# Nine score tiles turned by VectorE and a DRAM trip instead of TensorE, in a bucketed-attention and mixture-of-experts kernel

## The chip, the cores and the metric

The kernel runs on one core of a Trainium2 chip. The metric is device time in microseconds (us) of one execution, lower is better. The engines are named as the profile names them: PE is TensorE (PEld its weight load), DVE is VectorE, ACT is ScalarE, POOL is GpSimd, and SP is SyncE, whose queue issues nearly every DMA of this kernel. Each engine works through its own instructions in order.

## The reference

Two layers follow each other. The first is attention with a hash mask: a query sees only those keys whose six sign bits under a random projection are the same as its own. The second is a mixture of four experts over the attention's output, all experts computed for all rows and weighted by given probabilities.

```python
# q, k, v: (2, 8, 768, 64); proj: (64, 6); w1: (4, 512, 1024); w2: (4, 1024, 512)
q_bits = (np.einsum('bhsd,dk->bhsk', q, proj) > 0).astype(np.int64)
k_bits = (np.einsum('bhsd,dk->bhsk', k, proj) > 0).astype(np.int64)
q_bucket = np.sum(q_bits * powers, axis=-1)
k_bucket = np.sum(k_bits * powers, axis=-1)
mask = q_bucket[:, :, :, None] == k_bucket[:, :, None, :]
scores = np.where(mask, scale * np.matmul(q, k.transpose(0, 1, 3, 2)), -1000000000.0)
attn = np.exp(scores - np.max(scores, axis=-1, keepdims=True))
attn = attn / (np.sum(attn, axis=-1, keepdims=True) + 1e-09)
attn_out = np.matmul(attn, v)
...
x = attn_out.transpose(0, 2, 1, 3).reshape(B * S, H * D)
for e in range(E):
    h = np.maximum(x @ w1[e], 0.0)
    out += p[:, e:e + 1] * (h @ w2[e])
```

## The kernel before

**Tiles and steps.** There are 16 heads, (batch 0, heads 0 to 7) and then (batch 1, heads 0 to 7). A head's 768 queries are six tiles of 128. The attention is a software pipeline with one step per tile: at step i the tile i is scored, and operations on earlier tiles follow with fixed lags. In the text, t0 to t5 are the six steps in which a head's own tiles are scored. Inside a step the operations are written in the order T X S U V M E Y N R P:

- S (`stage_s`): four score matmuls on PE into a PSUM tile `sps` (two buffers), then on DVE a reduction over the scores (L432) that also writes them to the SBUF tile `p`.
- E, one step later: the exponential on ACT (L448).
- T, three steps after S (`stage_t`): the tile is turned by six 128x128 PE transposes (L493) into two PSUM tiles `ptps`; the first half is copied to SBUF by ACT (L499), the second by DVE where the tile is first or third of its group (L497), otherwise by ACT. Three tiles make a group, g = 0 and g = 1.
- X and Y, two and four steps after S (`stage_x`, `stage_y`): the other way to turn a tile. DVE transposes 32x32 blocks of the tile (L512), after three tiles one DMA writes the group (1152 KB) to a DRAM scratch `scr` (L518), and four DMAs of 288 KB read it back into `pt` in the wanted order (L529). SP waits for the write to land before it issues the reads.
- V (`stage_v`): the product with v, 12 matmuls (L547), in two parts of six pairs for a head of batch 0, at the lags LAG_V (4 and 6 steps after the head's last tile). Both groups of the head have to be there for either part.
- U: PSUM to SBUF by ACT (g = 0, L574) and DVE (g = 1, L572). N and R: reciprocals of the row sums on DVE, sent through DRAM (`row`) and spread over partitions into `rdb` (L473, one buffer, shared by a pair of heads). M (`stage_m`): three POOL operations per group on a pair's result: multiply by `rdb` (L585), then split into two float32r parts (L587, L590).
- P: steps of the generator `prep_head` for the next head: "hi" on ACT (L354) with copies on POOL (L242), "lo" on DVE (L357), "hash" on PE (`hps`, L369) with signs on ACT and two POOL copies (L384, L242). Loads of a later head's q, k (L216) and v (L232) and DVE's turn of a loaded q, k tile (L312) also stand here.

**Which way a tile goes.** `heavy(b, h, t)` chooses T for every tile of batch 0 and X and Y for every tile of batch 1.

**Stages.** Batch 0's attention runs first, beside the split of the first expert weights (casts L729 on DVE, subtractions L719 on POOL), which is paced by counting the yields of the attention generator. When batch 0 is done (126 us), PE goes over to the expert layers, and batch 1's attention is fed in between them. All PSUM tiles but `sps` share four buffers of one kind.

Of the kernel before, what the change touches and what calls it, by code (L numbers as in the profile page):

```python
# [21 lines left out]
SPLIT_AT = (1, 0)  # L22
# [9 lines left out]
LAG_M = (10, 10)  # L32
# [11 lines left out]
PREP_AT = 0  # L44
ORDER = "TXSUVMEYNRP"
LIGHT_FROM = 8
DRAIN = 2000
SPLIT_FIRST = 3
FAST = 6
# [3 lines left out]
def tile_lsh_attention__then__domain_moe(  # L53
# [24 lines left out]
    G = 3  # L78
# [235 lines left out]
    def prep_head(b, h):  # L314
        second = (b, h) == (0, 1)
        q1, al, ah, k2 = stack_tiles(b, h)

        def copies():
            for rows in (slice(0, D), slice(D, P)):
                copy_pool(q1[rows], ah[0:D].bitcast(F32))  # L320
            copy_pool(k2[0:D], ah[D:P].bitcast(F32))

        if second:
            for ps, sl in zip(in_psum, halves):
                nc.scalar.activation(ah[:, sl], ps[:, :NH], ACTF.Copy, scale=qk_scale)
            copies()
            yield 654
            for ps, sl in zip(in_psum, halves):
                low_half(al[:, sl], ps[:, :NH], ah[:, sl])
            yield 0  # L330
            yield 0
            ps = [one("hps1") for _ in range(2)]
            for j, (w, a) in enumerate(((phi, ah), (plo, ah), (phi, al))):
                for i, sl in enumerate(halves):
                    nc.tensor.matmul(ps[i][:MKE, :NH], w, a[:, sl], start=j == 0, stop=j == 2)
            copy_pool(ah[0:D], al[D:P].bitcast(F32))
            for i, sl in enumerate(halves):
                nc.scalar.activation(
                    k2[D:MKE, sl], ps[i][D:MKE, :NH], ACTF.Sign, bias=sgn_bias[D:MKE], scale=SGN_SCALE
                )  # L340
            yield 978
        else:
            xt = xts.pop((b, h))
            late = b * H + h > H
            steps = {}
            steps.setdefault(SPLIT_AT[late], []).append("hi")
            steps.setdefault(SPLIT_AT[late] + 1, []).append("lo")
            steps.setdefault(HASH_AT[late], []).append("hash")
            for at in range(max(steps) + 1):
                if at:  # L350
                    yield 654 if at == 1 else 0
                for what in steps.get(at, ()):
                    if what == "hi":
                        nc.scalar.activation(two(ah), two(xt), ACTF.Copy, scale=qk_scale)  # L354
                        copies()
                    elif what == "lo":
                        nc.vector.scalar_tensor_tensor(  # L357
                            out=two(al),
                            in0=two(xt),
                            scalar=qk_scale,  # L360
                            in1=two(ah).bitcast(F32),
                            op0=ALU.mult,
                            op1=ALU.subtract,
                        )
                        copy_pool(ah[0:D], al[D:P].bitcast(F32))
                    else:
                        hps = one("hps")
                        for i, sl in enumerate(halves):
                            nc.tensor.matmul(  # L369
                                hps[i * D : i * D + MKE - D, :NH],  # L370
                                pf[:, : MKE - D],
                                xt[:, sl],
                                start=True,
                                stop=True,
                                tile_position=(0, i * D),
                            )
                        for i, sl in enumerate(halves):
                            rows = slice(i * D, i * D + MKE - D)
                            nc.scalar.activation(
                                k2[D:MKE, sl], hps[rows, :NH], ACTF.Sign, bias=sgn_bias[rows], scale=SGN_SCALE  # L380
                            )
            if late:
                yield 978
        nc.gpsimd.tensor_scalar(  # L384
            out=al[D:MKE],
            in0=k2[D:MKE].bitcast(F32),
            scalar1=1.0,
            scalar2=bit_mul[D:MKE],
            op0=ALU.add,
            op1=ALU.mult,  # L390
        )
        copy_pool(k2[MQ:MQE], al[MK:MKE].bitcast(F32))
        yield 0 if second or b * H + h > H else 978
# [20 lines left out]
    def mixed(b, h):  # L414
        return b * H + h < LIGHT_FROM

    def heavy(b, h, t):
        return mixed(b, h)

    def stage_s(b, h, t):  # L420
        q1, q2, k1, k2 = heads[b, h]
# [177 lines left out]
    ready = [False]  # L599

    def v_lags(b, h):
        return LAST_V if (b, h) == (0, H - 1) else LAG_V[not mixed(b, h)]

    def u_lag(b, h):
        return v_lags(b, h)[-1] + (1 if (b, h) == (0, H - 1) else LAG_U[not mixed(b, h)])
# [4 lines left out]
    def attention():  # L610
        n = len(seq)
        prep = [iter(())]

        def do(op, i):
            if op == "N":
                j = i - LAG_N
                if 0 <= j < n:
                    stage_n(*seq[j])
            elif op == "R":
                for b in range(B):  # L620
                    for odd in range(2):
                        j = i - LAG_R[b][odd]
                        if 0 <= j < n and (seq[j][0], seq[j][1] % 2) == (b, odd):
                            stage_r(*seq[j])
            elif op == "T":
                j = i - LAG_T
                if 0 <= j < n and heavy(*seq[j]):
                    stage_t(*seq[j])
                    return 654
            elif op == "X":  # L630
                j = i - LAG_X
                if 0 <= j < n and not heavy(*seq[j]):
                    stage_x(*seq[j])
            elif op == "Y":
                j = i - LAG_Y
                if 0 <= j < n and j % G == G - 1 and not heavy(*seq[j]):
                    b, h, t = seq[j]
                    stage_y(b, h, t // G)
            elif op == "S":
                if i < n:  # L640
                    b, h, t = seq[i]
                    if t == 0:
                        x = hseq.index((b, h))
                        prep[0] = prep_head(*hseq[x + 1]) if x + 1 < len(hseq) else iter(())
                    stage_s(b, h, t)
                    return 652 + 4270 // NT
                return DRAIN
            elif op == "V":
                for bh, lag in ended(i):
                    for part, at in enumerate(v_lags(*bh)):  # L650
                        if lag == at:
                            stage_v(*bh, part, len(v_lags(*bh)))
                            if (bh, part) == ((0, H - 1), len(v_lags(*bh)) - 1):
                                ready[0] = True
                                return 0
            elif op == "U":
                for bh, lag in ended(i):
                    if lag == u_lag(*bh):
                        stage_u(*bh)
            elif op == "M":  # L660
                for (b, h), lag in ended(i):
                    for g in range(NT // G):
                        if h % 2 and lag == (u_lag(b, h) if (b, h) == (0, H - 1) else LAG_M[b] + g):
                            stage_m(b, h, g)
                if done_b[0] and ready[0]:
                    ready[0] = False
                    return 0
            elif op == "E":
                j = i - LAG_E
                if 0 <= j < n:  # L670
                    stage_e(*seq[j])
            elif op == "P":
                if i < n:
                    b, h, t = seq[i]
                    c = next(prep[0], None) if t >= PREP_AT else None
                    x = hseq.index((b, h))
                    if t == NT - 1 and x + 2 < len(hseq) and in_blocks(*hseq[x + 2]):
                        turn_blocks(*hseq[x + 2])
                    if t == QK_AT and x + 2 < len(hseq):
                        load_qk(*hseq[x + 2])  # L680
                    if t == NT - 1 and x + 1 < len(hseq):
                        load_v(*hseq[x + 1])
                    return c
            return None

        for i in range(n + LAG_M[1] + 3):
            for op in ORDER:
                c = do(op, i)
                if c is not None:
                    yield c  # L690
# [501 lines left out]
```

## Time and profile before

| what | value |
|---|---|
| median of 3 runs | 710.5 us (710.23 to 711.04) |
| the profiled execution's own time | 710.34 us |
| its span in the trace | 708.6 us |
| PE busy, share of the span | 700.9 us, 99% |
| DVE busy | 490.2 us, 69% |
| ACT busy | 333.6 us, 47% |
| POOL busy | 316.5 us, 45% |
| mean granted PE clock | 0.999 |

The shares are means over two stages with different work. PE's busy time counts matmuls that overlap each other, so 99% does not say that none of them waited. 1.7 us of the execution lie outside the span.

### The profile page before, as it was taken

The page shows a single profiled execution, that of the slowest core. Times are in us where ns is not written, and L with a number is a line of the kernel's source. Part 1 is how long each engine was busy: PE and PEld are TensorE (multiplying, and loading weights), DVE is VectorE, ACT ScalarE, POOL GpSimd, SP SyncE. Part 2 cuts the span into 40 slices and gives each one's busy share as a digit, 9 for nine tenths or more (in the row PEclk, how much of TensorE's full clock was granted, in tenths as well). Part 3 has the DMA queues.
Part 4 walks back from the last instruction along what each step waited for, and adds up shares of the span by engine and source line. Part 5 has one row for each costly group of instructions (what it writes and reads, how often), then busy time and mean ns, then how long its engine had stood idle before and what let it go on. Part 6 is the DMA issues. An engine that isn't in the chain of part 4 may idle for free.

```text
span 708.6 us, 10175 instructions
## 1 busy us (share of the span) xinstructions
PE 700.9 (99%) x3726; PEld 593.9 (84%) x3726; DVE 490.2 (69%) x782; ACT 333.6 (47%) x655; POOL 316.5 (45%) x290
## 2 busy tenths in 40 slices
PE   8999999999999999999999999999999999999997
PEld 6766675878887978978888989899898989989896
DVE  6898888865585754755228797886857667685762
ACT  6887788543453544524234444343433434353340
POOL 6359578523352453503238555543514234341420
PEclk9999999999999999999999999999999999999999
DMA  6323354768997977867931121421212121122202
GB/s 150 68 47 75 75 116 84 216 170 204 264 247 225 238 182 223 238 214 231 237 105 60 61 89 54 153 63 60 93 57 90 46 75 59 61 90 59 90 1 89
DMA packets 90848, 87.76 MB, mean 124 GB/s; under 512 B 53168, under 2 KB 55728, under 8 KB 90800
## 3 DMA queue, kind: packets, MB, share of 16 engines
q1 hardware_dynamic: 89776, 86.80, 44.2%
q8 instruction: 29, 0.48, 0.3%
q10 hardware_dynamic: 1024, 0.33, 0.2%
q14 instruction: 19, 0.16, 0.1%
HBM read 65.04 MB, written 22.07 MB: 123 GB/s over the span
## 4 chain that ended last, share of the span: by engine, by line
PE 93%; DVE 2%; POOL 2%; issue 1%; ACT 1%; DMA 0%; POOLq 0%; DVEq 0%
PE mps L760 12%; PE mps L762 12%; PE mps L761 12%; PE pv L547 8%; PE mps L808 5%; PE mps L810 5%; PE mps L809 5%; PE sps L427 4%; PE sps L425 4%; PE ptps L493 4%; PE mps L1051 3%; PE mps L1050 3%; PE mps L1047 3%; PE pa L1050 2%; PE pa L1051 2%; PE pd L1051 2%
## 5 line engine op out<-in xcount | busy, mean ns | idle before, releaser
L760 PE MATMUL mps<-w2hi,hh 128*128 128x512 f32 (+1 forms) x388 | 151.0, 389 | 0.0
L761 PE MATMUL mps<-w2lo,hh 128*128 128x512 f32 (+1 forms) x388 | 150.5, 388 | 0.0
L762 PE MATMUL mps<-w2hi,hl 128*128 128x512 f32 (+1 forms) x388 | 150.4, 388 | 0.0
L1033 POOL TENSOR_TENSOR w2lo<-ws,w2hi 128x512 fp32r<-128x512 f32 x40 | 50.7, 1287 | 124.0 <-ACT w2hi L1032 121.1
L432 DVE TENSOR_SCALAR_CACHE_REDUCE p<-sps 128x768 f32<-128x768 f32 x96 | 90.0, 939 | 17.8 <-PE sps L427 16.3
L754 DVE SCALAR_TENSOR_TENSOR acc<-mps,pe,acc 128x512 f32<-128x512 f32 (+1 forms) x85 | 62.9, 740 | 56.0 <-PE mps L762 55.7
L448 ACT ACTIVATE p<-p,nb 128x768 f32<-128x768 f32 x96 | 89.5, 933 | 23.4 <-DVE p L432 23.0
L762 PEld LDWEIGHTS mps<-w2hi,hl 128*128 128x128 f32 x388 | 72.9, 188 | 15.7
L760 PEld LDWEIGHTS mps<-w2hi,hh 128*128 128x128 f32 x388 | 72.8, 188 | 15.0 <-issue 1.2
L761 PEld LDWEIGHTS mps<-w2lo,hh 128*128 128x128 f32 x388 | 72.9, 188 | 14.0
L547 PE MATMUL pv<-pt,tv 128*64 128x384 f32 x288 | 67.1, 492 | 0.0
L992 POOL TENSOR_TENSOR w1lo<-ws,w1hi 128x512 fp32r<-128x512 f32 x30 | 47.5, 1589 | 41.9 <-ACT w1hi L988 41.7
L808 PE MATMUL mps<-xs,w1hi 128*128 128x384 f32 x192 | 65.1, 339 | 0.0
L810 PE MATMUL mps<-xs,w1lo 128*128 128x384 f32 x192 | 64.5, 336 | 0.0
L809 PE MATMUL mps<-xs,w1hi 128*128 128x384 f32 x192 | 64.5, 336 | 0.0
L843 ACT ACTIVATE hh<-mps 128x384 fp32r<-128x384 f32 x48 | 23.4, 489 | 84.6 <-PE mps L810 84.6
L1060 ACT ACTIVATE hh<-mt 128x384 fp32r<-128x384 f32 x60 | 31.5, 525 | 58.4 <-DVE mt L1105 38.0
L844 DVE SCALAR_TENSOR_TENSOR hl<-mps,hh 128x384 fp32r<-128x384 f32 x48 | 26.4, 554 | 46.0 <-ACT hh L843 45.7
L425 PE MATMUL sps<-ah,q 128*128 128x384 f32 x192 | 53.5, 359 | 0.4 <-DVE p L432 0.4
L547 PEld LDWEIGHTS pv<-pt,tv 128*64 128x64 f32 x288 | 24.9, 136 | 32.2 <-issue 30.7
L512 DVE STREAM_TRANSPOSE t<-p 128x768 f32<-128x768 f32 x48 | 46.3, 965 | 7.7 <-ACT p L448 7.6
L242 POOL TENSOR_SCALAR q<-ah 64x768 fp32r<-64x768 f32 (+1 forms) x33 | 27.1, 821 | 54.5 <-ACT ah L354 40.1
(160 smaller groups left out, 1528.6 us busy)
## 6 DMA issues: line engine op xcount, KB each, us to landing
ws<-in_moe_w_dram SPq DMA_DIRECT2D x64, 512.0 KB, 3.9
scr<-t SPq DMA_DIRECT2D x16, 1152.0 KB, 7.5
pt<-scr SPq DMA_DIRECT2D x64, 288.0 KB, 5.7
tv<-in_v_dram SPq DMA_DIRECT2D x16, 192.0 KB, 4.5
tqk<-in_q_dram SPq DMA_DIRECT2D x30, 96.0 KB, 3.3
out_dram<-acc SPq DMA_DIRECT2D x11, 256.0 KB, 2.0
tqk<-in_k_dram SPq DMA_DIRECT2D x28, 96.0 KB, 3.1
rdb<-row SPq DMA_DIRECT2D x14, 192.0 KB, 6.4
```

The source lines that it names most:

```text
L425: nc.tensor.matmul(ps[:, i, :NH], q1[:, sl], k1[:, i * NH : (i + 1) * NH], start=True, stop=False)
L432: nc.vector.tensor_scalar(out=two(pt), in0=ps[:, :, :NH], scalar1=MASKED, scalar2=MASKED, op0=ALU.min, op1=ALU.min, accum_out=nb,)
L448: nc.scalar.activation(pt, pt, ACTF.Exp, bias=nb, scale=-1.0, accum_out=dens[b, h, r][:, o : o + 1])
L547: nc.tensor.matmul(dst, vvs[b, h][:, c], pts[b, h, g][c], start=c == 0, stop=c == NT - 1, tile_position=(0, g * D),)
L754: nc.vector.scalar_tensor_tensor(out=acc, in0=ps, scalar=pcol, in1=acc, op0=ALU.mult, op1=ALU.add)
L760: nc.tensor.matmul(ps, hh[:, ts], w2hi[:, f, cs], start=n == 0, stop=False)
L761: nc.tensor.matmul(ps, hh[:, ts], w2lo[:, f, cs], start=False, stop=False)
L762: nc.tensor.matmul(ps, hl[:, ts], w2hi[:, f, cs], start=False, stop=n == FC - 1)
L808: nc.tensor.matmul(ps[:, :SB], w1hi[:, kk, fs], xhi[b, kk][:, sl], start=kk == 0, stop=False)
L809: nc.tensor.matmul(ps[:, :SB], w1hi[:, kk, fs], xlo[b, kk][:, sl], start=False, stop=False)
L810: nc.tensor.matmul(ps[:, :SB], w1lo[:, kk, fs], xhi[b, kk][:, sl], start=False, stop=kk == KD - 1)
L1033: nc.gpsimd.tensor_tensor(out=lo[:, c + o], in0=t[:, o], in1=hi[:, c + o].bitcast(F32), op=ALU.subtract)
```

## The change

In batch 0's heads 1, 3 and 5 the first group (tiles 0 to 2) goes by X and Y, the way of batch 1; their second group and all other heads stay with T. For these three heads the two parts of V move from 4 and 6 to 6 and 8 steps after the head's last tile, U follows at 11 instead of 9, and M at 11 and 12 instead of 10 and 11. For the head prepared during one of them (heads 2, 4 and 6), "hi" and "lo" come one step earlier, in t0 and t1.

```diff
+BY_BOTH = (1, 3, 5)
+LATE_V = (6, 8)
+LATE_M = 11
...
-            steps.setdefault(SPLIT_AT[late], []).append("hi")
-            steps.setdefault(SPLIT_AT[late] + 1, []).append("lo")
+            at = 0 if by_both(b, h - 1) else SPLIT_AT[late]
+            steps.setdefault(at, []).append("hi")
+            steps.setdefault(at + 1, []).append("lo")
...
+    def by_both(b, h):
+        return b == 0 and h in BY_BOTH
+
     def heavy(b, h, t):
-        return mixed(b, h)
+        return mixed(b, h) and not (by_both(b, h) and t < G)
...
     def v_lags(b, h):
+        if by_both(b, h):
+            return LATE_V
         return LAST_V if (b, h) == (0, H - 1) else LAG_V[not mixed(b, h)]
+
+    def m_lag(b, h):
+        return LATE_M if by_both(b, h) else LAG_M[b]
...
-                        if h % 2 and lag == (u_lag(b, h) if (b, h) == (0, H - 1) else LAG_M[b] + g):
+                        if h % 2 and lag == (u_lag(b, h) if (b, h) == (0, H - 1) else m_lag(b, h) + g):
```

Three places show how instructions move. Line numbers of the changed kernel are 3 to 12 higher than those of the kernel before, and numbers at a name's end are buffer numbers. The first place is PE in head 3, from the hash matmuls of t3 to the scores of t5, before:

```order
L369 MATMUL hps<-xt,pf 44x384 x2
L493 MATMUL ptps<-ident,p 128x128 x6
L425 MATMUL sps<-ah,q_540 128x384 x2
L427 MATMUL sps<-k_543,al 128x384 x2
L493 MATMUL ptps<-ident,p 128x128 x6
L425 MATMUL sps<-ah,q_540 128x384 x2
L427 MATMUL sps<-k_543,al 128x384 x2
```

The same place in the changed kernel:

```order
L373 MATMUL hps<-xt,pf 44x384 x2
L432 MATMUL sps<-ah,q_520 128x384 x2
L434 MATMUL sps<-k_523,al 128x384 x2
L432 MATMUL sps<-ah,q_520 128x384 x2
L434 MATMUL sps<-k_523,al 128x384 x2
```

The two sixes of transposes are gone (a third, ahead of t3, too), and three groups of score matmuls come close together.

The second place is DVE in head 3, from the second reduction (t1) to the fourth (t3), before:

```order
L432 TENSOR_SCALAR p,nb<-sps 128x768
L497 COPY pth<-ptps 128x3x128
L432 TENSOR_SCALAR p,nb<-sps 128x768
L729 CAST w1hi<-ws 128x512
L572 COPY xr<-pv 64x384
L459 TENSOR_SCALAR den<-den 128x6
L460 RECIPROCAL rd<-den 128x6
L357 SCALAR_TENSOR_TENSOR al<-xt,qk_scale,ah 128x768
L497 COPY pt<-ptps 128x3x128
```

In the changed kernel DVE has from there to the reduction of t5 (t_739 is the tile `t1` of `stage_x`):

```order
L361 SCALAR_TENSOR_TENSOR al<-xt,qk_scale,ah 128x768
L504 COPY pth<-ptps 128x3x128
L519 STREAM_TRANSPOSE t_739<-p 128x6x4x32
L439 TENSOR_SCALAR p,nb<-sps 128x768
L466 TENSOR_SCALAR den<-den 128x6
L467 RECIPROCAL rd<-den 128x6
L519 STREAM_TRANSPOSE t_739<-p 128x6x4x32
L439 TENSOR_SCALAR p,nb<-sps 128x768
L741 CAST w1hi<-ws 128x512
L519 STREAM_TRANSPOSE t_739<-p 128x6x4x32
L439 TENSOR_SCALAR p,nb<-sps 128x768
L579 COPY xr<-pv 64x384
```

A block transpose now stands ahead of each of three reductions, "lo" stands a step earlier, and the two copies of this group are gone.

The third place is the queue of SP between two loads of q and k, at the end of head 3, before:

```order
L462 DMA row<-rd 128x6
L473 DMA rdb<-row 64x768
L232 DMA tv<-in_v_dram 128x384
L708 DMA ws<-in_moe_w_dram 128x2x512
L216 DMA tqk<-in_q_dram 32x24x32 x2
```

The same place in the changed kernel:

```order
L469 DMA row<-rd 128x6
L525 DMA scr<-t_739 128x4x576
L480 DMA rdb<-row 64x768
L235 DMA tv<-in_v_dram 128x384
L536 DMA pt<-scr 32x4x576 x4
L219 DMA tqk<-in_q_dram 32x24x32 x2
```

The write of the group stands ahead of the DMA into `rdb`, the four reads behind it and behind the load of v; the load of expert weights has moved away from here.

## Rows read from the trace of the kernel before

**Rows 1.** Page, part 2: busy tenths in 40 equal slices.

```profile
PE   8999999999999999999999999999999999999997
...
DVE  6898888865585754755228797886857667685762
```

**Rows 2.** Windows, one per head from its first scores: heads 2, 3, 4; mean of 1 to 7.

```profile
core 0: us, PE busy (x) PEld busy (x) DVE busy (x) ACT busy (x) POOL busy (x), PEclk, DMA share, GB/s
...
32.11:45.74 13.63, 13.63 (x91) 9.49 (x89) 12.57 (x25) 11.36 (x25) 6.64 (x8) 1.00 0.28 60
45.74:59.38 13.64, 13.64 (x91) 9.49 (x90) 12.44 (x25) 11.49 (x25) 8.92 (x9) 1.00 0.19 29
59.38:73.64 14.26, 13.91 (x92) 9.46 (x90) 11.10 (x21) 11.32 (x25) 11.61 (x12) 1.00 0.48 122
...
sum 96.58, PE 95.97 PEld 66.41 DVE 83.70 ACT 79.78 POOL 62.17; mean PE 13.71 PEld 9.49 DVE 11.96 ACT 11.40 POOL 8.88
```

**Rows 3.** Timeline of PE, head 3 and start of head 4: start, us, line, count.

```profile
49.24 0.96 PE L493 MATMUL ptps<-ident,p 128*128 128x128 f32 x6
49.97 0.60 PE L425 MATMUL sps<-ah,q 128*128 128x384 f32 x2
...
50.84 0.54 PE L547 MATMUL pv<-pt,tv 128*64 128x384 f32 x1
...
52.82 0.82 PE L369 MATMUL hps<-xt,pf 128*44 128x384 f32 x4
53.57 0.87 PE L493 MATMUL ptps<-ident,p 128*128 128x128 f32 x6
54.20 0.59 PE L425 MATMUL sps<-ah,q 128*128 128x384 f32 x2
...
54.98 1.05 PE L493 MATMUL ptps<-ident,p 128*128 128x128 f32 x6
55.78 0.60 PE L425 MATMUL sps<-ah,q 128*128 128x384 f32 x2
...
60.33 0.62 PE L427 MATMUL sps<-k,al 76*128 76x384 f32 x2 [0.35 <-POOL k L242]
```

**Rows 4.** Groups of lines by form, 10 to 140 us: count | busy, mean ns | idle before.

```profile
L499 ACT ACTIVATE pth<-ptps 128x384 f32<-128x384 f32 x32 | 14.7, 487 | 8.5 <-PE ptps L493 8.5
...
L497 DVE COPY pt<-ptps 128x384 f32<-128x384 f32 x16 | 8.8, 553 | 0.2
...
L512 DVE STREAM_TRANSPOSE t<-p 128x768 f32<-128x768 f32 x7 | 6.7, 961 | 0.0
```

**Rows 5.** Timeline of DVE, head 3: the reduction of t4.

```profile
55.18 0.96 DVE L432 TENSOR_SCALAR_CACHE_REDUCE p<-sps 128x768 f32<-128x768 f32 x1 [0.46 <-PE sps L427]
```

**Rows 6.** Timeline of PE, head 4: the scores of t5.

```profile
70.03 0.60 PE L425 MATMUL sps<-ah,q 128*128 128x384 f32 x2
```

**Rows 7.** Timeline of SP: the first two trips through scr, of batch 1.

```profile
126.77 0.38 SPq L518 DMA_DIRECT2D scr<-t  x1
...
132.74 1.75 SPq L529 DMA_DIRECT2D pt<-scr  x4
136.84 0.38 SPq L518 DMA_DIRECT2D scr<-t  x1
...
144.43 1.74 SPq L529 DMA_DIRECT2D pt<-scr  x4
```

**Rows 8.** Line L529, 130 to 140 us, then 140 to 150 us: issue to landing.

```profile
DMA to landing us min/median/max: 3.2/4.5/5.7
...
DMA to landing us min/median/max: 4.4/5.6/6.5
```

**Rows 9.** Timelines of POOL and SP, end of head 3: a pair's multiplications and rdb.

```profile
61.60 1.20 POOL L585 TENSOR_TENSOR xr<-xr,rdb 128x384 f32<-128x384 f32 x1
...
51.90 0.33 SPq L462 DMA_DIRECT2D row<-rd  x1
62.82 0.48 SPq L473 DMA_DIRECT2D rdb<-row  x1
```

## Prediction

> **What bounds the kernel now.** I read the page by slices first. PE is at 9 tenths in nearly every slice; DVE stands at 8 or 9 tenths in the first seven slices, some 125 us, and at 5 to 8 later [rows 1]. The change is in that first stage, batch 0's attention, so I cut it by heads. A head takes 13.80 us on average (96.58 over seven heads), PE is busy in practically all of it, and DVE in 11.96, which leaves DVE 1.84 us of idle time per head; the granted clock is 1.00 throughout [rows 2]. The timeline of PE shows what a head is made of. The six transposes of one tile take 0.63 to 0.80 us from their start to the next scores; one half of the product with v takes 1.98 us (50.84 to 52.82), the hash matmuls 0.75 [rows 3]. So PE sets the pace of this stage, and DVE is second with 13% to spare. Behind the stage PE goes on into the expert layers at 9 tenths of every slice, so time saved ahead of them should come out at the end.
>
> **The change, part by part.**
>
> *PE loses nine sets of six transposes.* In head 3 the three that go are 49.24 to 49.97, 53.57 to 54.20 and 54.98 to 55.78: 0.73 + 0.63 + 0.80 = 2.16 us [rows 3]. Heads 1 and 5 have the same pattern, so PE loses about 6.5 us. Moving V removes nothing from PE: it stands two steps later, in t5 of the following head and t1 of the one after. A pair of heads (an odd one and the even one that follows) takes 27.6 us now and would be 25.4 for PE alone.
>
> *ACT loses copies.* Four copies per group at 0.487 us go, 1.9 us per odd head [rows 4]. ACT is not the bound (11.4 of 13.8 us [rows 2]), so I count nothing.
>
> *DVE gains.* It gets three block transposes of 0.961 us and loses two copies of 0.553: +1.78 us per odd head [rows 4]. The block transpose of batch 0 is not in this trace; that of batch 1 has the same form, and I take it unchanged. The pair needs 2 x 11.96 + 1.78 = 25.7 us of DVE [rows 2, 4]. That is more than PE's 25.4: the limit moves from one engine to the other, and of the 2.16 us that PE gives up at most 27.6 - 25.7 = 1.9 can be had per pair, 5.7 in all.
>
> *What the coupling takes.* That floor holds only if DVE never idles. It does idle whenever PE stands in V or hash and neither of the two score tiles in PSUM is waiting for it. Bounds: no idle time, and twice that of the head where DVE is densest now, head 2 with 13.63 - 12.57 = 1.06 us [rows 2]. With "lo" and the reductions placed as in the order above, DVE has work queued during most of PE's long blocks, so I take the middle, 1.06 us per pair: 26.76, a gain of 0.83 per pair and 2.5 us for three. The two ends give 5.7 and, at 2.1 us of idle time, -0.6.
>
> *"hi" and "lo" a step earlier, M a step later.* DVE's work does not change by it, only its place. On POOL it puts the copies of head 4's k ahead of the multiplications of heads 0 and 1. Now PE waits for that copy at the start of head 4, 0.35 us of it seen as idle time [rows 3], and head 4 takes 0.62 us more than head 3 [rows 2]. I count 0.5 us gained; 0 to 0.62 is possible.
>
> *The trip through DRAM.* This is new in this stage, with a wait that PE can feel: the matmuls of V need the read-back tile, and behind them in PE's order stand the next head's transposes and scores, on which DVE waits. Time available: the third block transpose stands ahead of the reduction of t4, which is at 55.18 now [rows 5]; V will stand behind the scores of t5 of the next head, at 70.03 + 0.87 (the distance of 49.97 to 50.84 [rows 3]) = 70.9 [rows 6]. From these 15.7 us go one half of V that moves out of the stretch (1.98), one set of transposes (0.80) and the wait for POOL (0.5): 12.4, and up to 1 us less when DVE runs late. I take 12. Time needed: from the issue of the write to the reads' issue 5.97 us (126.77 to 132.74) in the one trip that meets little other traffic, 7.6 in the next one (136.84 to 144.43) [rows 7]; then 1.75 us for four issues, of which the slowest lands 5.7 and 6.5 us after its own issue [rows 8]. That makes 11.7 to 13.4 us for the first trip, as the slowest is the first or the last of the four, and 14.1 to 15.8 for the second. Stage one moves less (DMA share 0.19 to 0.48 [rows 2]), so the first trip is the nearer one: V comes out just in time or a little late. One thing is worse than in batch 1: in SP's queue the DMA into `rdb` stands between write and reads, and it has to wait until POOL has multiplied the pair before. Now that wait holds SP from 52.2 to 62.82, until the multiplication that starts at 61.60 is done [rows 9]. Head 1 has no pair before it, so nothing; heads 3 and 5 I give 0.5 us each, -1.0 in all. The bounds are 0 and 3.8 (15.8 against 12) per head.
>
> *The other DMAs* (one write and four reads per odd head, ahead of a load of q and k that is needed a head later) cost SP 0.38 + 1.75 us of issue [rows 7], in a queue that stands idle for 10 us [rows 9]: nothing.
>
> **Sum.** 2.5 + 0.5 - 1.0 = 2.0 us off the profiled execution's 710.34 (span 708.6, with 1.7 outside it): 708.3. The median of the runs is 0.16 above that execution, so 708.4 for the median.
>
> **A rule that speaks against it.** In the rows, a tile's turn costs PE 0.63 to 0.80 and DVE 0.37 on average by the old way, and DVE 0.96 by the new one. The Trainium skill ("VectorE: DVE Perf Modes", section "Rules for kernel authors") advises TensorE for a 128x128 transpose whose result may go to PSUM, and DVE's transpose only inside 32x32 blocks. Taken as the deciding rule, the work would stay on PE, and the change would give nothing or lose; that is the first rival, whose price follows from the rows.
>
> **Rivals.**
>
> 1. *DVE takes it all.* If DVE keeps about the idle time that it has now around PE's long blocks, two times 0.95 us per pair instead of 1.06, a pair takes 25.7 + 1.9 = 27.6, as before, and the kernel 710.4, within 0.2% (1.4 us, about what a measurement of this kernel can tell from no change). For it: DVE and PE would be within 0.3 us of each other, and only two score tiles lie between them. Against: today's 1.84 us per head arises while DVE waits for a slower PE, which it then would not.
> 2. *The product with v waits for its tile.* Slower from the point where the wait is over 1 us per head (three heads against 2.5 + 0.5 gained). If `rdb` holds the reads back as it holds SP now and the reads meet traffic as in the second trip, the wait is 2 to 3.8 us per head; with 2.5 on three heads, 7.5 - 3.0 = 4.5 slower, 715; with 2.5 on heads 3 and 5 alone, 2.0 slower, 712.5. For it: 12 against 11.7 leaves nothing in reserve. Against: the earlier "hi" brings POOL's copies out of the way of the multiplication.
> 3. *The trip is hidden and DVE does not idle.* Then 5.7 + 0.5 are gained: 704.3. For it: the odd and even heads would be balanced on both engines. Against: an idle time of zero is in no window of the stage.
>
> **How the numbers follow.** The forecast (a gain of 0.5 to 4 us) gets 0.50, the first rival 0.25, the second 0.17, the third 0.08. A quarter of the forecast's weight lies under 1.4 us, and a little of the first rival's above: faster by over 0.2% 0.52, within 0.2% 0.28, slower 0.20. The range reaches down to most of the third case and up to the mild form of the second: 704.9 to 711.9; the forecast's own is 706.4 to 709.9.
>
> **What would show it.** In the profile after, the windows by head should give about 26.8 us for a pair, DVE busy in over 95% of it, and PE's score matmuls waiting for DVE's reduction (L439). The wait of head 4's score matmuls for POOL should be gone. The waits of PE's weight loads for V (L554) should name a DMA from `scr` for 0 to 1 us in heads 3 and 5 and none in head 1. The prediction is wrong if that wait is over 1 us per head, if a pair takes over 27.3 with DVE short of 95%, or if the expert stage, from its first matmul to the end, gets longer by what the first stage gave.

## The result and the profile after

The changed kernel takes 720.7 us (median of 4 runs, 720.40 to 721.26); the kernel before took 710.5 on the same chip. The ratio is 1.0143, with a 95% interval of 1.0126 to 1.0161. The forecast was 708.4 us with a range of 704.9 to 711.9: it is 12.3 us too low, and the kernel moved the other way. The profiled execution took 720.91 us, its span is 719.2.

Line numbers of the changed kernel are 3 to 12 higher than before: S is L432 and L434, the reduction L439, T L500, the block transpose L519, the write to `scr` L525, the reads L536, V L554, `rdb` L480, POOL's multiplication L592.

The page's slices (40 of 18 us) of PE and of its granted clock already have the place:

```profile
PE   8997979999999999999999999999999999999997
...
PEclk9998989999999999999999999999999999999999
```

PE falls to 7 tenths in the fourth and sixth slice, and the clock behind it, in the fourth and sixth too. The windows by head, which answer to [rows 2], say which heads (here heads 3 to 7, and the sum over 1 to 7):

```profile
core 0: us, PE busy (x) PEld busy (x) DVE busy (x) ACT busy (x) POOL busy (x), PEclk, DMA share, GB/s
...
44.05:57.73 13.68, 13.68 (x86) 8.43 (x84) 13.26 (x25) 10.03 (x21) 7.98 (x8) 1.00 0.40 103
57.73:76.40 18.67, 13.42 (x79) 9.24 (x78) 12.75 (x23) 11.38 (x25) 14.13 (x15) 0.82 0.76 162
76.40:89.98 13.58, 13.58 (x86) 8.46 (x84) 12.14 (x23) 9.93 (x21) 6.52 (x7) 1.00 0.66 167
89.98:108.93 18.95, 14.51 (x79) 9.88 (x77) 13.01 (x26) 11.59 (x25) 14.29 (x15) 0.83 0.69 141
108.93:125.62 16.69, 15.84 (x103) 10.43 (x101) 11.75 (x24) 11.67 (x25) 9.38 (x11) 0.99 0.29 56
sum 106.90, PE 94.99 PEld 63.73 DVE 86.63 ACT 75.96 POOL 63.24; mean PE 13.57 PEld 9.10 DVE 12.38 ACT 10.85 POOL 9.03
```

The sum was 96.58: these seven heads account for 10.3 of the 10.6 us between the two spans. What follows them is unchanged: from head 8's first scores to the end it is 719.2 - 125.62 = 593.6 us, before 708.6 - 115.08 = 593.5. Heads 4 and 6 take 4.4 and 5.0 us more than before, though each holds one half of V (2.08 us) less, and their granted clock is 0.82 and 0.83. Head 7 takes 3.15 us more, but about 2 of that is one half of V [rows 3], which the later lag has moved from the front of this stretch to its end.

PE's timeline shows the wait in head 4 and the same in head 6, at the first half of V:

```profile
68.03 0.62 PE L434 MATMUL sps<-k,al 76*128 76x384 f32 x2
72.34 0.87 PE L554 MATMUL pv<-pt,tv 128*64 128x384 f32 x1 [3.68 <-DMA pt<-scr]
...
103.70 0.87 PE L554 MATMUL pv<-pt,tv 128*64 128x384 f32 x1 [3.29 <-DMA pt<-scr]
```

V waited 3.68 and 3.29 us for the reads from `scr`; in head 2, for head 1's tile, there is no such wait. Why the reads were late stands in SP's timeline, which answers to [rows 7, 9]:

```profile
55.31 0.38 SPq L525 DMA_DIRECT2D scr<-t  x1
62.34 0.49 SPq L480 DMA_DIRECT2D rdb<-row  x1
62.93 0.53 SPq L235 DMA_DIRECT2D tv<-in_v_dram  x1
63.56 1.79 SPq L536 DMA_DIRECT2D pt<-scr  x4
```

and in POOL's:

```profile
61.10 1.21 POOL L592 TENSOR_TENSOR xr<-xr,rdb 128x384 f32<-128x384 f32 x1
```

SP issues the write at 55.31 and stands until 62.34, when POOL has multiplied the pair before (61.10 + 1.21 = 62.31). The write itself landed 4.3 us after its issue, at about 60, so it was not what SP still stood for. Only then come `rdb`, the load of v and the reads, whose last landed 7.32 us after its issue at 64.93. For head 5's tile it is the same: write at 86.87, `rdb` at 93.23 just behind POOL's multiplication, reads at 94.47.

The windows of 2 us around the first wait show a second price, in the column PEclk, ahead of the DMA share:

```profile
66.00:68.00 2.00, 1.20 (x8) 1.06 (x9) 1.97 (x5) 1.29 (x4) 1.84 (x3) 1.00 1.05 214
68.00:70.00 2.00, 0.65 (x4) 0.22 (x2) 1.74 (x5) 1.94 (x5) 1.92 (x3) 0.57 1.06 225
70.00:72.00 2.00, 0.00 (x0) 0.00 (x0) 0.00 (x0) 0.00 (x0) 1.81 (x3) 0.50 1.26 189
72.00:74.00 2.00, 1.66 (x6) 0.85 (x8) 0.00 (x0) 0.00 (x0) 0.64 (x1) 0.50 0.85 89
74.00:76.00 2.00, 2.00 (x10) 0.74 (x7) 0.98 (x1) 0.00 (x0) 0.00 (x0) 0.72 0.73 146
```

The granted clock falls to 0.50, the 1.2 GHz level, and stays there when PE works again. In windows of 0.2 us the fall in head 4 lies between 68.2 and 68.4, while PE was still busy with the scores (to 68.65): ahead of the wait for V, and behind a wait of 1.57 us for an eviction by VectorE. In head 6 it lies at 102.4, 2.0 us into the wait for V.

```profile
66.80 0.85 PE L500 MATMUL ptps<-ident,p 128*128 128x128 f32 x6 [1.57 <-DVE pt L504]
```

The chain of waits has what the half products took at that clock (start, duration, what):

```profile
64.93 7.32 DMA pt<-scr
72.25 0.09 issue
72.34 3.50 PE pv L554 x12
...
103.70 4.11 PE pv L554 x12
107.81 1.48 PE ptps L500 x6
```

3.50 and 4.11 us where a half takes about 2 at full clock, and 1.48 for a set of transposes that takes 0.6 to 0.8 [rows 3].

### The profile page after: what moved, and what is told of

It reads as the page before. It is cut to its first block, busy times and chain, and to the rows that moved or that the text cites. A ratio compares the mean times of both kernels' runs of the same rounds, so it can differ in the third digit from the quotient of the medians.

```text
span 719.2 us, 10098 instructions
## 1 busy us (share of the span) xinstructions
PE 700.1 (97%) x3672; PEld 591.2 (82%) x3672; DVE 494.2 (69%) x785; ACT 329.7 (46%) x643; POOL 317.1 (44%) x290
## 4 chain that ended last, share of the span: by engine, by line
PE 92%; DMA 2%; DVE 2%; ACT 2%; issue 0%; SPq 0%; ACTq 0%; DVEq 0%
PE mps L772 12%; PE mps L774 12%; PE mps L773 12%; PE pv L554 9%; PE mps L820 5%; PE mps L822 5%; PE mps L821 5%; PE sps L432 4%; PE sps L434 4%; PE ptps L500 3%; PE mps L1063 3%; PE mps L1062 3%; PE mps L1059 3%; DMA pt<-scr 2%; PE pa L1062 2%; PE pa L1063 2%
## 5 line engine op out<-in xcount | busy, mean ns | idle before, releaser
L439 DVE TENSOR_SCALAR_CACHE_REDUCE p<-sps 128x768 f32<-128x768 f32 x96 | 89.5, 934 | 14.5 <-PE sps L434 14.0
L774 PEld LDWEIGHTS mps<-w2hi,hl 128*128 128x128 f32 x388 | 72.9, 188 | 15.7
L554 PE MATMUL pv<-pt,tv 128*64 128x384 f32 x288 | 70.3, 504 | 7.2 <-DMA pt<-scr 7.0
L519 DVE STREAM_TRANSPOSE t<-p 128x768 f32<-128x768 f32 x57 | 54.9, 964 | 7.9 <-ACT p L455 7.7
L554 PEld LDWEIGHTS pv<-pt,tv 128*64 128x64 f32 x288 | 25.8, 140 | 40.3 <-issue 38.4
L432 PE MATMUL sps<-ah,q 128*128 128x384 f32 x192 | 53.5, 360 | 0.9 <-DVE p L439 0.9
```

Source lines behind the costliest of these rows:

```text
L432: nc.tensor.matmul(ps[:, i, :NH], q1[:, sl], k1[:, i * NH : (i + 1) * NH], start=True, stop=False)
L439: nc.vector.tensor_scalar(out=two(pt), in0=ps[:, :, :NH], scalar1=MASKED, scalar2=MASKED, op0=ALU.min, op1=ALU.min, accum_out=nb,)
L519: nc.vector.transpose(out=t1v[:, :, o].rearrange("p r c q -> p c r q"), in_=pt.rearrange("p (c r k) -> p c r k", c=NT, r=QD),)
L554: nc.tensor.matmul(dst, vvs[b, h][:, c], pts[b, h, g][c], start=c == 0, stop=c == NT - 1, tile_position=(0, g * D),)
L774: nc.tensor.matmul(ps, hl[:, ts], w2hi[:, f, cs], start=False, stop=n == FC - 1)
```

## The experiments

Four theories were to be told apart. A: the reads are held in SP's queue behind `rdb`, and the clock adds to the wait. B: the trip through DRAM is too long for the moved V whatever stands in the queue. C: VectorE has become the bound and takes the gain. D came up on the way: moving V unbalances odd and even heads. Each time is a median; each kernel was timed beside the kernel before, which had 710.3 to 710.5.

**1. `rdb` behind the reads** (e1_r_later). The load of `rdb` for heads 0, 2 and 4 comes two steps later and so stands behind the reads in SP's queue.

```diff
+LATE_R = 8
+    def r_lag(b, h):
+        return LATE_R if by_both(b, h + 1) else LAG_R[b][h % 2]
...
-                        j = i - LAG_R[b][odd]
-                        if 0 <= j < n and (seq[j][0], seq[j][1] % 2) == (b, odd):
-                            stage_r(*seq[j])
+                        for lag in (LAG_R[b][odd], LATE_R):
+                            j = i - lag
+                            if 0 <= j < n and (seq[j][0], seq[j][1] % 2) == (b, odd):
+                                if r_lag(*seq[j][:2]) == lag:
+                                    stage_r(*seq[j])
```

> The load of rdb for heads 0, 2 and 4 is issued two steps later, so that in SP's queue it stands behind the four reads of the turned tile and no longer ahead of them. Theory A (the queue): the reads of heads 3 and 5 started late, at 63.56 and 94.47 us, only because rdb, ahead of them, waited for POOL's multiplication of the pair before (it ended at 62.31 and 93.21). With the order turned round they start about 5 us earlier, the product with v of heads 3 and 5 waits under 1 us on them, PE's granted clock stays at 1.00 behind it, and the two pairs give back about 4.5 us each: 711 to 713 us. Rival B (the trip itself): write, landing, reads and landing take longer than the steps between the last X and the product, whatever stands in the queue; the waits of 3.3 to 3.7 us shrink by less than 1 us and the time is 718 to 721 us. Rival C (VectorE took over the work and is the bound): the waits go, but the pairs stay at 27.4 us or above, 711 us and not below 710.

Measured: 711.7 us, ratio to the kernel before 1.0018 (1.0008 to 1.0027). SP's timeline (line numbers one higher):

```profile
55.15 0.38 SPq L526 DMA_DIRECT2D scr<-t  x1
...
59.85 3.53 SPq L537 DMA_DIRECT2D pt<-scr  x4
63.49 0.49 SPq L481 DMA_DIRECT2D rdb<-row  x1
```

PE's timeline at the first half of V in head 4:

```profile
67.90 0.52 PE L435 MATMUL sps<-k,al 76*128 76x384 f32 x2
68.48 0.51 PE L555 MATMUL pv<-pt,tv 128*64 128x384 f32 x1
```

The windows of head 4, and the sum of all seven:

```profile
57.57:71.20 13.63, 11.98 (x79) 8.80 (x78) 12.05 (x24) 11.39 (x25) 12.94 (x14) 1.00 0.91 191
...
sum 97.30, PE 91.36 PEld 61.83 DVE 86.35 ACT 76.03 POOL 63.05; mean PE 13.05 PEld 8.83 DVE 12.34 ACT 10.86 POOL 9.01
```

The reads start at 59.85, when the write has landed, and V goes on at 68.48 with no wait for a DMA. The clock is 1.00 in all seven heads, also behind a wait of 1.59 us in head 4 for the same eviction. One place in a queue was worth 720.7 - 711.7 = 9.0 us. Theory A is shown, B is out. C is not touched by this run: it had expected 711 us as well.

**2. No trip** (e2_no_trip).

```diff
     def stage_x(b, h, t):
...
+        if by_both(b, h):
+            if o == G - 1:
+                flat = turned.pop((b, h, g)).rearrange("p t s -> p (t s)")
+                px = flat.rearrange("p (a c q) -> p c a q", c=NT, q=32)
+                pts[b, h, g] = [px[:, c] for c in range(NT)]
+            return
```

> Leaves out the write of the turned tile to DRAM and its reads; the product with v reads what VectorE's block transposes left, so the rearrangement is missing from the output of these heads. It shows the engines' part alone: 8 block transposes for a head on VectorE, 8 x 8 fewer transposes on PE, fewer evictions on ACT and VectorE. If the prediction's sum of the engines holds (26.8 us for a pair against 27.6), 708 us, with VectorE above 95% busy. If VectorE takes the gain (rival 1 of the prediction), 710 to 711 us. If the loss of the change were not in the trip at all but in the load on the engines or the moved steps, it stays above 715 us.

(A turned head has three block transposes in place of 18 on PE; the counts of 8 are a slip.) Measured: 711.4 us, ratio 1.0013 (1.0003 to 1.0022). With no trip at all the engines' part gives nothing over the whole stage. The run is no clean price of that part, however: in head 4 PE waited 1.58 us for an eviction by VectorE, the clock fell there to 0.51 as well, and the head took 14.86 us where it had taken 13.63 in the first experiment. PE's timeline, then the window of 2 us:

```profile
65.97 1.45 PE L500 MATMUL ptps<-ident,p 128*128 128x128 f32 x6 [1.58 <-DVE pt L504]
```

```profile
66.00:68.00 2.00, 2.00 (x9) 2.00 (x10) 2.00 (x5) 1.31 (x4) 1.92 (x3) 0.51 0.92 155
```

**3. Head 1 alone** (e3_head1).

```diff
-BY_BOTH = (1, 3, 5)
+BY_BOTH = (1,)
```

> Only head 1 goes by VectorE and DRAM. In the changed kernel its reads were not held up: rdb of the first pair waits for nothing, and its product with v did not wait. Theory A (rdb held behind POOL's multiplication of the pair before): no wait, 710 to 711 us, since pair 1 measured 25.3 us only because half a product with v (2.1 us) slid out of it. If every head so turned costs a third of the 10.2 us, 714 us. If pair 1 truly gains the 1.9 us that its period shows, 708.6 us.

Measured: 711.1 us, ratio 1.0006 (0.9997 to 1.0015). Turning head 1, whose `rdb` waits for nothing, costs and gains nothing that can be measured, with what its moved V does in heads 2 and 3 included. The loss is not a price of each turned head.

**4. The moved steps alone** (e4_lags_only).

```diff
     def heavy(b, h, t):
-        return mixed(b, h) and not (by_both(b, h) and t < G)
+        return mixed(b, h)
```

> All tiles are turned by PE again; of the change only the moved steps stay: the product with v of heads 1, 3 and 5 two steps later, its eviction and POOL's multiplications with it, and the splits of heads 2, 4 and 6 from the first step on. Theory A: the moved steps alone cost next to nothing, 710 to 712 us; the wait of the scores on POOL at head 4 stays away. Rival: the later product with v and multiplications of POOL push the next pair's work by themselves (rdb waits for POOL here too), then 714 us or more.

Measured: 718.5 us, ratio 1.0113 (1.0098 to 1.0128). The rival's number came where theory A had expected 710 to 712: with PE turning all tiles, the moved steps cost 8.0 us. Theory D comes from this run.

**5. Only V and what follows it late** (e6_v_late_only). As the last, and:

```diff
-            at = 0 if by_both(b, h - 1) else SPLIT_AT[late]
+            at = SPLIT_AT[late]
```

> All tiles turned by PE; the product with v of heads 1, 3 and 5 two steps later, its eviction and POOL's multiplications with it, and the splits of heads 2, 4 and 6 back at their old steps. It tells apart which of the moved steps cost the 8.0 us of the run with all of them. Theory D (balance): a half of the product with v (2.08 us of PE) goes from each even head to the odd head behind it, which then holds three; odd heads come to 16.55 us with PE full, and in even heads PE waits for VectorE and ScalarE. Then the cost stays: 717 to 719 us. Rival: the early splits put VectorE's and ScalarE's work at a bad place; then 711 to 713 us.

Measured: 718.3 us, ratio 1.0107 (1.0092 to 1.0122): the early splits are innocent; the later V, with U and M that follow it, costs the 8 us. The windows of heads 2, 4 and 5 show how:

```profile
32.36:47.55 15.19, 13.55 (x80) 9.18 (x78) 12.78 (x25) 11.37 (x25) 6.64 (x8) 0.89 0.29 54
...
64.10:76.95 12.85, 12.02 (x79) 8.62 (x78) 11.73 (x24) 11.43 (x25) 10.55 (x11) 1.00 0.55 123
76.95:93.50 16.55, 15.70 (x104) 10.29 (x102) 11.06 (x23) 11.78 (x25) 8.10 (x10) 1.00 0.28 64
```

At lags 4 and 6 both halves of a head's V lie in the next head. At 6 and 8 the second half of an odd head's V lies in the head after the next, an odd one again. So from head 3 on an odd head's time has three halves and 15.7 us of PE's work, an even one's one half, and PE is idle 0.8 us in either. That is only a part of the loss. With the moved half product (2.08 us) counted where it went, heads 3 to 6 lose 3.1 of the 7.6 us that the seven heads lose in this trace, head 7 0.9, and head 2 alone 3.6: there PE waited 0.72 and then 0.92 us for VectorE, the clock fell to 0.50, and the head took 15.19 us with one half of V where it had taken 13.63 with two.

```profile
42.29 0.62 PE L432 MATMUL sps<-ah,q 128*128 128x384 f32 x2 [0.92 <-DVE p L439]
```

In the changed kernel the turned odd heads have lost the transposes that make room for the third half; head 7, which is not turned, has not.

**6. The wait filled** (e5_fill, e9_fill_half). To part the wait from the clock, the wait is filled with multiplications whose sums are overwritten.

```diff
+N_FILL = 12
...
+        if part == 0 and by_both(b, h) and h > 1:
+            for c in range(N_FILL):
+                nc.tensor.matmul(
+                    ps[D:P, :GN].rearrange("p (a q) -> p a q", q=32),
+                    vvs[b, h][:, c % NT],
+                    pts[b, h, 1][c % NT],
+                    start=True,
+                    stop=True,
+                    tile_position=(0, D),
+                )
```

> The changed kernel, with 12 more multiplications of TensorE ahead of the first half of the product with v of heads 3 and 5, on tiles that are there already; their sums are overwritten, so the output is the same. They fill the stretch in which PE waited 3.68 and 3.29 us for the reads, and last about as long (12 x 0.34 = 4.1 us). Theory A (what the wait costs is more than its length: behind it the granted clock stood at 0.50 to 0.72 and the half products took 3.50 and 4.11 us in place of 2.08): the waits stay in the form of this filling, the clock stays at 1.00, and the kernel is faster than the changed kernel by 3 to 4 us, 717 us. Rival: the halves were slow for another reason (their operands, the reads' traffic), or the added work costs what the clock gives back: 720 to 722 us.

Measured: 725.6 us, ratio 1.0218 (1.0203 to 1.0233), a miss of the dose: the 24 instructions took about 8 us, twice the wait. With 5 in place of 12:

> The filling again, with 5 multiplications in place of 12. One lasted 0.69 us and not 0.34 (two instructions for each, 24 in 8.2 us), so that 12 of them outlasted the wait by 4.5 to 5 us for each head. Five take 3.4 us, a little less than the waits of 3.68 and 3.29 us. Theory A (the clock adds to the wait): the half products take 2.1 us again, and the kernel is at 716 to 717.5 us, 3 to 4.5 below the changed kernel. Rival (the clock costs nothing of its own): 720 to 721 us.

Measured: 716.9 us, ratio 1.0096 (1.0080 to 1.0113). PE's timeline in head 4:

```profile
68.30 3.44 PE L551 MATMUL pv<-pth,tv 128*64 128x384 f32 x10
72.30 0.54 PE L565 MATMUL pv<-pt,tv 128*64 128x384 f32 x1 [0.56 <-DMA pt<-scr]
```

The window of 2 us behind the filling, PEclk ahead of the DMA share:

```profile
72.00:74.00 2.00, 1.70 (x12) 0.77 (x12) 0.03 (x1) 0.00 (x0) 0.46 (x1) 1.00 0.83 95
```

V starts at 72.30, as late as in the changed kernel, but at full clock. The work that fills the wait makes the kernel 720.7 - 716.9 = 3.8 us faster, 1.2 of it in head 4 (17.47 for 18.67 us) and 2.65 in head 6 (16.30 for 18.95). So the 9.0 us are about 3.8 of clock and 5.2 of waiting. The 3.8 is an upper bound of what the hold itself cost by the clock: in head 6 V started 0.3 us earlier after the head's first scores, and in head 4 the clock had fallen ahead of the wait for V.

**7. Where V stands, with the hold gone** (e7_thirds, e8_both_at_6, e12_head5_at_6). All three have `rdb` later, as in the first experiment.

```diff
-LATE_V = (6, 8)
+LATE_V = (6, 6, 8)
```

> The kernel with the later load of rdb, and the product with v of heads 1, 3 and 5 in thirds: two at the sixth step behind the head, one at the eighth. PE's work in odd heads falls from 13.68 to 12.99 us and in even heads rises from 12.0 to 12.7; VectorE's is 13.46 and 12.05. Theory D (balance): PE's idle time in even heads, 1.6 us each, shrinks by 0.5 to 1.0 and the kernel takes 708.5 to 710.5 us. Rival C (VectorE has no room in either head of a pair): 711 to 712 us.

Measured: 710.5 us, ratio 1.0005 (0.9996 to 1.0015): 1.1 us less than in the first experiment, at the upper end of what theory D expected.

```diff
-LATE_V = (6, 8)
+LATE_V = (6, 6)
```

> The kernel with the later load of rdb, and both halves of the product with v of heads 1, 3 and 5 at the sixth step behind the head: each head holds two halves again, as before the change. Theory D (balance): odd heads have PE at 11.6 us and VectorE at 13.4, even heads PE at 14.0; VectorE idles while the 4.2 us of products stand between two score tiles, and head 7 falls back by 2 us: 709 to 711 us. Rival: the reads' landing, just in time for the half at this step, now holds up both halves: 712 us or more.

Measured: 714.1 us, ratio 1.0053 (1.0038 to 1.0068), a miss, and not by the reads. With two halves only, PE in head 3 has long gaps in which it waits for VectorE's reduction, and the clock falls to 0.50 for the next 6 us: the head takes 17.50 us. Head 5, turned too and with two halves, has such a gap as well, but the clock stayed at 1.00 and the head took 13.54 us.

```profile
53.37 0.62 PE L433 MATMUL sps<-ah,q 128*128 128x384 f32 x2 [0.75 <-DVE p L440]
...
56.24 1.01 PE L433 MATMUL sps<-ah,q 128*128 128x384 f32 x2 [1.90 <-DVE p L440]
...
87.63 0.62 PE L433 MATMUL sps<-ah,q 128*128 128x384 f32 x2 [1.72 <-DVE p L440]
```

So a turned head with two halves has PE waiting for VectorE, and the third half fills PE there; but nearly all of the miss is the slow clock in head 3. With head 3 at head 5's 13.54 the run would be at 710 us (an estimate), where theory D had put it.

```diff
-            return LATE_V
+            return LATE_V if h < BY_BOTH[-1] else (6, 6)
```

> The kernel with rdb later and the product with v in thirds, and head 5's product in two halves at the sixth step, so that head 7, which PE turns alone and which has no block transposes, no longer carries a part of it. Theory D (balance): head 7 falls from 15.9 to 13.55 us, head 6 rises from 13.7 to 15.2 or less: 709.5 to 710 us. Rival C (VectorE has no room in the pair): what head 7 loses head 6 gains, 710.5 us or more.

Measured (with thirds for heads 1 and 3): 709.4 us, ratio 0.9987 (0.9978 to 0.9996). Head 7 is back at 13.54 us, head 6 goes to 15.02. This version beats the changed kernel and, by 0.13%, the kernel before.

**8. What still holds PE** (e11_all_early, e10_two_to_act). Both start from the last kernel.

```diff
-            at = 0 if by_both(b, h - 1) else SPLIT_AT[late]
+            at = 0 if by_both(b, h - 1) or by_both(b, h) or (b, h) == (0, H - 1) else SPLIT_AT[late]
```

> As the run with head 5 at the sixth step, and the splits of heads 1, 3, 5 and 7 from the first step on as well. In the kernel in thirds PE waited 0.2 to 1.0 us in heads 4 and 6, four times, for evictions that stood on VectorE behind the subtraction of the low halves (1.81 us at 64.38). Theory D: with the subtraction a step earlier these waits go, about 1 us for a pair: 707 to 709 us, faster than before. Rival C (the work on VectorE has to be done, wherever it stands): no change, 709.5 to 710.5 us.

Measured: 709.45 us, ratio 0.9985 (0.9976 to 0.9994), against 709.44: no change, as C had expected; theory D had put it at 707 to 709.

```diff
-            if i and o % 2 == 0:
+            if i and o % 2 == 0 and not (by_both(b, h - 1) and t == 0 or by_both(b, h) and t == NT - 1):
```

> As the run with head 5 at the sixth step, with two of VectorE's evictions of each pair (of head 2's, 4's, 6's first tile and of head 1's, 3's, 5's last) on ScalarE. VectorE loses 1.1 us for a pair, ScalarE gains 0.95. If VectorE alone bounds the pair (rival C): 1 us less for a pair, 707 to 708.5 us. If PE waits for VectorE and ScalarE alike, since both are packed in the same two steps of the even heads: no gain, 709.5 to 711 us.

Measured: 709.8 us, ratio 0.9987 (0.9978 to 0.9996): no gain. Two of PE's waits in head 4 are at the same places, with the other engine's name. With head 5 at the sixth step, and then with two evictions moved to ScalarE:

```profile
62.89 0.55 PE L501 MATMUL ptps<-ident,p 128*128 128x128 f32 x3 [0.54 <-DVE pth L505]
...
67.07 0.85 PE L501 MATMUL ptps<-ident,p 128*128 128x128 f32 x6 [0.66 <-DVE pt L505]
```

```profile
63.30 0.55 PE L501 MATMUL ptps<-ident,p 128*128 128x128 f32 x3 [0.59 <-ACT pth L507]
...
67.82 0.55 PE L501 MATMUL ptps<-ident,p 128*128 128x128 f32 x3 [0.64 <-ACT k L384]
```

Over the seven heads VectorE had 2.9 us less to do (83.65 us busy in place of 86.51), and PE waited as long, for ScalarE. Neither engine alone is the bound in the even heads; both are full in the same two steps: in the run with head 5 at the sixth step neither VectorE nor ScalarE has a gap of 0.1 us from 60.7 to 67.5. A third wait in head 4, ahead of V, is put down to ScalarE in the one run (0.62 us) and to a read from `scr` in the other (0.63), so there the trip is again only just in time.

## Why the prediction was wrong, by its own steps

The forecast gain of 2.0 us and the measured loss of 10.2 are some 12 us apart. 8.0 of them are the trip's: a loss of 1.0 was forecast for it, and the hold alone measured 9.0. The other 4.2 are the engines' and POOL's: a gain of 3.0 was forecast, and with the hold gone the kernel lost 1.2.

*The step that failed* is "heads 3 and 5 I give 0.5 us each". The prediction had the hold: it quoted SP standing until POOL's multiplication was done [rows 9]. But its "time needed" counted from the write, 11.7 to 13.4 us, on trips of batch 1 whose reads nothing holds, and the hold entered only as "one thing is worse". Reckoned from the hold's end, 62.82, with 0.48 for `rdb`, up to 1.31 for the issues ahead and a landing of 5.7 to 6.5 us [rows 7 to 9], the reads would have landed at 69.0 to 71.1, 2 to 4 us after V was ready (55.18 + 12 = 67.2). The trip itself was sized right: without the hold it is over within the 13.3 us from 55.15 to 68.48.

*"The earlier hi brings POOL's copies out of the way of the multiplication"* was the argument against the second rival. The copies did go, but the change also puts M a step later, and POOL had other work ahead; the multiplication ended at 62.31, where it had ended at 62.80 [rows 9]. That rival, with 0.17, named the right mechanism in the right heads. Its price, 2.5 us per head, was too small for the waits of 3.68 and 3.29, which lie inside its own 2 to 3.8, and had no term for the clock.

*The clock* stands in no step, because it was 1.00 in every window of before [rows 2]. It cost about 3.8 us.

*The engines, 2.5 us of gain,* measured a loss of about 1 (711.7 with the hold gone, 711.4 without the trip). The parts were right: the block transpose took 0.96 us, PE's work in head 3 without the third half fell by 2.0 us, and a pair needs 25.5 us of VectorE (13.46 + 12.05 in the first experiment; 25.7 forecast). Wrong was the idle time beside it, 1.06 us per pair: the first experiment's pair of heads 3 and 4 took 27.31 us, so 1.8, and that of heads 5 and 6 27.70 (0.79 of it a wait for POOL at the start of head 5). "A pair takes over 27.3 with DVE short of 95%" was the prediction's own sign of failure, and it came. The reason is a sentence in the sum, "Moving V removes nothing from PE": true of its amount, but each odd head's time then has PE full with three halves, each even head's has PE waiting for evictions, and the average over the pair, which the sum used, does not exist in either. The moved half took the room that the transposes had made.

The largest loss of the engines' part lies in a head that the sum left out: head 7, which PE turns alone and which got a third half, took 17.01 us for 13.54, 1.4 more than the half product. The two pairs still gained in the first experiment, 0.6 and 0.2 us (27.90 each before). Without the trip the pair of heads 5 and 6, at a clock of 1.00, took 13.58 + 13.08 = 26.66, where 26.8 was forecast, with 24.9 us of VectorE instead of 25.7.

```profile
71.74:85.32 13.58, 13.58 (x86) 8.47 (x84) 12.14 (x23) 9.92 (x21) 6.61 (x8) 1.00 0.32 73
85.32:98.40 13.08, 11.92 (x80) 8.70 (x78) 12.79 (x26) 11.39 (x25) 12.31 (x14) 1.00 0.37 79
```

Thirds and head 5's V at one step gave back 2.2 us, which makes the engines' part about 1 us of gain in place of 2.5.

*The first rival* (VectorE takes it all, 710.4) was thus nearer the truth for the engines, and the rule cited beside it, the Trainium skill's "VectorE: DVE Perf Modes", section "Rules for kernel authors", is borne out to that extent: moving these transposes to VectorE was worth 0.13% to 0.15% in the best arrangements tried. That VectorE alone was the bound was not shown; the last experiment speaks against it.

*Right were* the end of head 4's wait for POOL (its score matmuls follow each other without a wait, 57.73 and 58.16; with the hold gone, a wait of 0.79 us for POOL came at the start of head 5 instead), no wait for head 1's tile, and an unchanged expert stage.

*Open* is the split of the last microsecond of the engines' part between VectorE, ScalarE and the order of their work, and why the clock fell in head 4 of the changed kernel: it did so ahead of the wait for V, and behind the same wait for an eviction it stayed at 1.00 in the first experiment.

## What to carry to other kernels

In SP's queue a DMA that waited for another engine held the ready ones behind it; so reckon a new transfer's start from the end of the longest wait ahead of it in the queue, and put loads that nobody needs yet behind those that TensorE will wait for. When work is moved by whole blocks between alternating stretches, sum each stretch by itself: a mean over the pair hides a full engine in the one and a waiting engine in the other. A wait on TensorE can cost more than its length where its clock falls beside it: here about 3.8 us more, for two waits.

## What was not expected of the hardware

TensorE's granted clock fell to the 1.2 GHz level beside waits of 1.6 to 3.7 us in the changed kernel and in the run without the trip, and behind 0.72 and 0.92 us in head 2 of the runs with the moved steps alone; in the changed kernel the next half product took 3.50 and 4.11 us. The Trainium skill ("TensorE: Matmul & The Clock Gate", section "What's actually happening") says that the throttled clock is the default and activity releases it; the filling with 5 agrees, with 1.00 throughout. But work after a wait does not always prevent the fall: in head 4 of the changed kernel it came 1.5 us after PE had taken up work again (66.80 to about 68.3), and in the run with 12 multiplications PE had waited 1.58 us at 67.1, was busy without a gap from then on, and the clock was still 0.73 and 0.50 in the two windows after it.

```profile
68.00:70.00 2.00, 2.00 (x6) 0.95 (x7) 2.00 (x5) 2.00 (x4) 1.89 (x3) 0.73 1.06 228
70.00:72.00 2.00, 2.00 (x5) 0.77 (x4) 0.04 (x2) 0.24 (x2) 1.89 (x2) 0.50 1.19 190
```

With 5 multiplications, and in the first experiment, the same wait of 1.6 us brought no fall. Whether a gap of that length costs the clock differed here between nearly the same programs.
